# Spectral mixing plus gated linear unit on one core: the third and fourth sums of the transform blocks made by accumulating DMAs of GpSimd

## The chip, the cores and the metric

One core of a Trainium2 chip. Its engines run side by side and each works through its own instructions in order: TensorE (PE, matrix products into PSUM), VectorE (DVE, elementwise), ScalarE (ACT, here copies and the layer norm's roots), GpSimd (POOL, here almost only the issue of DMAs), SyncE (SP, issue of DMAs only). Sixteen DMA engines move the data; POOL's DMAs go through one queue (q0 of the profile), SP's through another (q1). The metric is the device time of one execution in microseconds.

## What is computed

```python
def _A_ref(x, dft_seq_re, dft_seq_im, dft_hid_re, dft_hid_im):
    a = jnp.einsum("bsd,ed->bse", x, dft_hid_re)
    b = jnp.einsum("bsd,ed->bse", x, dft_hid_im)
    y = jnp.einsum("ts,bse->bte", dft_seq_re, a) - jnp.einsum("ts,bse->bte", dft_seq_im, b)
    return y

def _B_ref(x, W_gate, W_up, W_down):
    gate = jnp.einsum("bsd,df->bsf", x, W_gate)
    up = jnp.einsum("bsd,df->bsf", x, W_up)
    gate = gate * (gate > 0)
    return jnp.einsum("bsf,fd->bsd", gate * up, W_down)

xn = _layernorm(x, axis=-1)
return x + _A_ref(xn, ...) + _B_ref(xn, ...)
```

Here x is 2048 tokens by 640, the sequence transforms are 2048 by 2048, and W_gate and W_up are 640 by 1728; everything is float32. The change lies in the product of the sequence transforms (`dft`) with the normalized tokens.

## The kernel before

**Precision.** Every float32 operand is split into a high part, a copy rounded to fp32r on ACT, and a low part, the difference, on DVE (`split`, L124 to L126). A product is three matmuls, L131 to L133. A matmul has a moving operand of 512 columns.

**Fewer products.** The product of the transforms with the tokens is a 2 by 2 block product, with the real and imaginary transform as one pair of blocks and the two halves of the tokens as the other. It is done with seven block products in place of eight (the scheme of Strassen and Winograd). For that, sums of transform blocks are needed, called T1 to T4, beside the plain blocks B11, B21 and B22. The sums of token blocks are made once, in `sums_124` and `sums_3`. The sums of results are made in `combine`.

**Chunks and units.** The 2048 output tokens are four chunks (c = 0 to 3) of 512. After the products of B11 and B21 for all chunks comes the stream of chunks 0 to 3. A chunk is twenty units: T1, T2, B22, T3 and T4, each for g = 0 to 3 (256 tokens of the half each). T31 is below the unit of T3 with g = 1. The units of a chunk run in the order T10 T11 T12 T13 T20 B220 T21 B221 T22 T23 B222 B223 T30 T31 T32 T33 T40 T41 T42 T43. A unit of T1 or B22 has 18 matmuls on PE, one of T2, T3 or T4 has 12.

A unit (`stream`) has a load, a preparation and its products. The load brings one or two transform blocks of 512 KB by SP (`get`, L690): for T1 the block (0, 0) into a `raw` tile and (1, 0) into a `tk` tile, `TK[g]`, for T2 the block (1, 1) into a `raw` tile, `ST[g]`; T3 loads (0, 0) a second time and T4 (0, 1), each into a `raw` tile of its own. The preparation subtracts on DVE (L686): T1 leaves its difference in `TK[g]`, T2 replaces it by `ST[g] - TK[g]`, T3 and T4 put the difference with `TK[g]` into their own `raw` tile, and B22 takes `ST[g]` as it is. Then the result is split into `cb`, of which there are three buffers. There are six `raw` and four `tk` buffers. So the next chunk's `tk` load (`tk<-in_dft`) waits for the last use of `TK[g]`, which is T4's subtraction.

**What sets the order.** `drive` goes through the list of units: the load of a unit runs some units ahead of its preparation, the preparation two units ahead of the products. `defer(n, f)` calls f n units later. A scheduler then lays out each engine's instructions by modelled times, so that steps can change places with those of neighbouring units; the order on an engine is fixed when the kernel is built.

**What else runs there.** For the second part of the kernel, token sets are made in the stream of chunks 0 to 2 (`token_sets`, six steps): POOL loads `rows` and `in_xt` into `st` tiles (L409, L410, L426, L427), DVE works on them (L432 to L439), and POOL stores them into `set1` (L416, L448), two stores of 512 KB for each of the last four steps. SP later loads sets back (`st<-set`, L762), and ACT and DVE split them into `r1` (`r<-st`). POOL also loads `sa` (L707) and stores the chunk's results (`pq`, L659). All DMAs of POOL stand in one order, and so do those of SP.

```python
                tc.keep_in_program_order(tt(part(ab, i), part(ab, i), part(mr, 0), op=OP.add))
...
            for i, st in ((B11, t["ab"]), (T1, t["mr"])):
                nc.gpsimd.dma_start(sets[q][i : i + 4, :, cs].rearrange("i p t -> p i t"),
                                  st.rearrange("p (i t) -> p i t", i=4))
```

Of the kernel before, what the change touches and what calls it, by code (L numbers as in the profile page):

```python
# [10 lines left out]
OP = mybir.AluOpType  # L11
# [10 lines left out]
NH = NG // 2  # L22
# [13 lines left out]
B11, B12, B21, B22, T1, T2, T3, T4, X4 = range(9)  # L36
# [23 lines left out]
def fnet_reglu_kernel(  # L60
# [15 lines left out]
    nc = tc.nc  # L76
# [41 lines left out]
    def stage():  # L118
        return stages[-1].tile([P, W2], F32, name="st")

    def copy(o, i):
        return nc.scalar.activation(o, i, AF.Copy)  # L122

    def split(hi, lo, src):  # L124
        nc.scalar.activation(hi, src, AF.Copy)  # L125
        return nc.vector.tensor_tensor(lo, src, hi.bitcast(F32), op=OP.subtract)  # L126
# [11 lines left out]
    @contextmanager  # L138
    def in_turn():

        with ExitStack() as order:
            if len(lows) > BACK:
                order.enter_context(tc.issue_after(lows[-BACK].ins))
            yield
# [5 lines left out]
    def defer(units, f):  # L150

        deferred.setdefault(now[0] + units, []).append(f)
# [300 lines left out]
    def raw():  # L453
        return raw_p.tile([P, W2], F32, name="raw")

    def parts():
        return ring.tile([P, 2, SG, CH], F32R, name="cb")

    def flat(t, v):
        return t[:, v].rearrange("p j t -> p (j t)")  # L460

    def s4_part(g):

        if "s4" not in late:
            late["s4"] = get_gw0().rearrange("p v z -> p (v z)")
        b = g * SG * 2 * HC
        return late["s4"][:, b : b + SG * 2 * HC].rearrange("p (j v d) -> p j v d", j=SG, v=2)

    def sums_124(g):


        def make():
            both = lambda g, cs: [xn_block(g, cs, v) for v in range(2)]
            a11, a21, a12, a22 = both(g, K1), both(g, K2), both(g + NH, K1), both(g + NH, K2)
            s1, s2 = (i.rearrange("p (j d) -> p j d", j=SG) for i in (lambda t: (t[:, :CH], t[:, CH:]))(stage()))
            w = s4_part(g)
            tt = nc.vector.tensor_tensor
            f = lambda i: i.bitcast(F32)
            tc.keep_in_program_order(tt(s1, f(a21[0]), f(a22[0]), op=OP.add))
            tt(s1, s1, f(a22[1]), op=OP.add)  # L480
            tt(s2, s1, f(a11[0]), op=OP.subtract)
            tt(s2, s2, f(a11[1]), op=OP.subtract)
            split(*a21, s1)

            tt(s1, f(a12[0]), s2, op=OP.subtract)
            tt(s1, s1, f(a12[1]), op=OP.add)
            split(*a11, s2)
            split(w[:, :, 0], w[:, :, 1], s1)

        todo.append((idle, make, idle, idle))  # L490
# [19 lines left out]
    E, F, TK, ST = {}, {}, {}, {}  # L510
# [40 lines left out]
    def resident(g, d):  # L551
        return lambda j, i: xn_part(g * SG + j, d + i)

    def fourth(g):
        return lambda j, i: tuple(s4_part(g)[:, j, v, i * P : (i + 1) * P] for v in range(2))

    def add(o, i0, i1):
        return nc.vector.tensor_tensor(o, i0, i1, op=OP.add)  # L558

    def minus(o, i0, i1):  # L560
        return nc.vector.scalar_tensor_tensor(o, i0, -1.0, i1, op0=OP.mult, op1=OP.subtract)  # L561

    def sums_a():
        return sums.tile([P, 3, CH], F32, name="sa")

    def sums_b():
        return sums.tile([P, 4, CH], F32, name="sb")
# [86 lines left out]
    def combine(c, name):  # L654

        a, b = F["a"], F.get("b")
        if name == "T1":
            F["b"] = b = sums_b()
        store = lambda m, at, t: defer(1, lambda: nc.gpsimd.dma_start(pqd[c][m][:, at : at + t.shape[1]], t))  # L659
        for i in range(2):  # L660
            p1, p5, u2 = a[:, i], b[:, i], b[:, 2 + i]
            e1, e2 = (E.get((k, i)) for k in ("e1", "e2"))
            if name == "T1":
                copy(p5, e2)
            if name == "T2":
                minus(u2, e1, p1)
            if name == "B22":
                nc.vector.tensor_tensor(u2, u2, e2, op=OP.subtract)
            if name == "T3":
                add(p1, e1, p1)  # L670
                minus(p5, p5, p1)
            if name == "T4":
                add(p1, e2, p1)
        if name == "B22":
            v = a[:, 2]
            minus(v, E["v2"], v)
            store(1, 0, b[:, 2:4])
            store(1, 2, a[:, 2:3])
        if name == "T3":
            store(1, 3, b[:, :2])  # L680
        if name == "T4":
            store(0, 3, a[:, :2])

    def stream(c, name, g):
        t = {}
        sub = lambda o, i0, i1: nc.vector.tensor_tensor(o, i0, i1, op=OP.subtract)  # L686

        def get(m, half, o=None):
            o = raw() if o is None else o
            late["dma"] = nc.sync.dma_start(o, dft[c, m, half * NH + g]).ins  # L690
            return o

        def load():
            if name == "T1":
                t["s"] = get(0, 0)
                TK[g] = get(1, 0, tk.tile([P, W2], F32, name="tk"))
            elif name == "T2":
                ST[g] = get(1, 1)
            elif name == "T3":
                t["s"] = get(0, 0)  # L700
            elif name == "T4":
                t["s"] = get(0, 1)

        def prepare():
            if name == "T2" and g == 0:
                F["a"] = sums_a()
                nc.gpsimd.dma_start(F["a"], firsts[c])  # L707
            src = t.get("s", TK[g])
            with in_turn():
                if name == "T1":  # L710
                    src = TK[g]
                    sub(src, src, t["s"])
                elif name == "T2":
                    sub(src, ST[g], src)
                elif name == "B22":
                    src = ST[g]
                elif name == "T3":
                    sub(src, TK[g], src)
                elif name == "T4":

                    sub(src, src, TK[g])
                t["b"] = b = parts()
                lows.append(split(flat(b, 0), flat(b, 1), src))

        def run():
            b = t["b"]
            es = lambda n: [(n, 0), (n, 1)]
            if name == "T1":
                product(g, b, resident(g, 2), es("e2"), True, False, ("v2", 0, True))
            elif name == "T2":  # L730
                product(g, b, resident(g, 0), es("e1"), True, False)
            elif name == "B22":
                product(g, b, fourth(g), es("e2"), False, True, ("v2", 1, False))
            elif name == "T3":
                product(g, b, resident(g + NH, 0), es("e1"), False, True)
            else:
                product(g, b, resident(g + NH, 2), es("e2"), True, False)

        todo.append((load, prepare, run, lambda: combine(c, name) if g == NH - 1 else None))

    def set_parts(q, i):
# [96 lines left out]
    tt = nc.vector.tensor_tensor  # L838
# [527 lines left out]
```

## Time and profile before

| | us |
|---|---|
| median of 3 runs (1026.6 to 1027.81) | 1027.18 |
| span of the profiled execution | 1025.6 |
| PE busy | 1019.3 (99%) |
| DVE busy | 805.5 (79%) |
| ACT busy | 448.2 (44%) |
| POOL busy | 96.9 (9%) |
| DMA queue of SP, share of the 16 engines | 47.9% |
| DMA queue of POOL, share of the 16 engines | 18.9% |

The span is what one profiled execution took from its first to its last instruction; the runs are timed from outside, and their median is 1.6 us above it. Times within the execution (as "314.15") count from the span's start. The streams of chunks 1, 2 and 3 lie at about 190 to 255, 255 to 320 and 320 to 385 us. In the rows of a timeline the brackets give the time for which the engine stood idle before the instruction and what ended it. Busy times don't say what waits for what; for that the chain of waits and the timelines are read.

### The profile page before, as it was taken

How to read it: one execution, taken by the hardware profiler on the slowest of the kernel's cores; microseconds unless marked ns; L12 is line 12 of the kernel's file. 1: busy time of each engine (PE TensorE's matmuls, PEld its weight loads, DVE VectorE, ACT ScalarE, POOL GpSimd, SP SyncE). 2: the span in 40 equal slices, each digit the busy share in tenths (PEclk: the TensorE clock that was granted, in tenths of full speed). 3: DMA queues.
4: the chain of work that ended last, by engine and by line, in shares of the span. 5: the costliest groups of instructions: out<-in, count | busy, mean ns of one | idle time of the engine just before them, and what ended most of it. 6: DMA issues, size and time to landing. Idle time of an engine off the chain costs nothing.

```text
span 1025.6 us, 12560 instructions
## 1 busy us (share of the span) xinstructions
PE 1019.3 (99%) x4525; PEld 843.1 (82%) x4525; DVE 805.5 (79%) x1113; ACT 448.2 (44%) x571; POOL 96.9 (9%) x161
## 2 busy tenths in 40 slices
PE   9999999999999999999999999999999999999998
PEld 7888888888888888888888888888888888888886
DVE  7967976969888797787887888876586779777776
ACT  6664453333334443433335544443454434553442
POOL 2000010121110001421110000000000001000000
PEclk9999999999999999999999999999999999999999
DMA  9884744976869665863474666664595747994655
GB/s 327 321 283 157 264 152 138 338 246 208 350 205 336 228 197 196 265 229 135 172 242 146 224 216 226 236 226 170 198 357 188 254 145 237 385 337 140 218 172 160
DMA packets 104542, 236.45 MB, mean 231 GB/s; under 512 B 11936, under 2 KB 55328, under 8 KB 102944
## 3 DMA queue, kind: packets, MB, share of 16 engines
q1 hardware_dynamic: 86896, 165.49, 47.9%
q0 software_dynamic: 17152, 69.74, 18.9%
q8 instruction: 35, 0.57, 0.2%
q10 hardware_dynamic: 432, 0.43, 0.1%
q14 instruction: 27, 0.22, 0.1%
HBM read 179.50 MB, written 55.07 MB: 229 GB/s over the span
## 4 chain that ended last, share of the span: by engine, by line
PE 97%; DVE 2%; DMA 0%; ACT 0%; issue 0%; SPq 0%; ACTq 0%
PE ps L132 31%; PE ps L131 31%; PE ps L133 31%; PE ps L519 3%; PE ps L548 1%; PE ps L1250 1%; DVE cb L126 1%; DMA raw<-in_dft 0%; DVE raw L686 0%; DVE r L126 0%; DVE sb L561 0%; DVE sa L558 0%; DVE tk L686 0%; ACT cb L125 0%; ACT cb L349 0%
## 5 line engine op out<-in xcount | busy, mean ns | idle before, releaser
L133 PE MATMUL ps<-cb,wt 128*128 128x512 f32 x412 | 160.0, 388 | 0.0
L132 PE MATMUL ps<-cb,wt 128*128 128x512 f32 x412 | 159.9, 388 | 0.0
L131 PE MATMUL ps<-cb,wt 128*128 128x512 f32 x412 | 159.8, 388 | 0.0
L125 ACT ACTIVATE cb<-rw 128x1024 fp32r<-128x1024 f32 x83 | 81.9, 987 | 121.7 <-PE ps L133 105.8
L126 DVE TENSOR_TENSOR cb<-rw,cb 128x1024 fp32r<-128x1024 f32 x83 | 94.0, 1132 | 50.9 <-ACT cb L125 50.5
L125 ACT ACTIVATE cb<-raw 128x1024 fp32r<-128x1024 f32 x64 | 67.8, 1060 | 103.7 <-PE ps L133 94.8
L126 DVE TENSOR_TENSOR cb<-raw,cb 128x1024 fp32r<-128x1024 f32 x64 | 78.2, 1221 | 31.9 <-ACT cb L125 31.6
L131 PE MATMUL ps<-xs_early,gw 128*128 128x512 f32 x260 | 101.1, 389 | 0.0
L132 PE MATMUL ps<-xs_early,gw 128*128 128x512 f32 x260 | 101.1, 389 | 0.0
L133 PE MATMUL ps<-xs_early,gw 128*128 128x512 f32 x260 | 101.1, 389 | 0.0
L133 PEld LDWEIGHTS ps<-cb,wt 128*128 128x128 f32 x412 | 77.3, 188 | 16.1 <-DVE wt L126 0.3
L131 PEld LDWEIGHTS ps<-cb,wt 128*128 128x128 f32 x412 | 77.3, 188 | 16.1
L132 PE MATMUL ps<-cb,xs_late 128*128 128x512 f32 x232 | 90.5, 390 | 0.1
L132 PEld LDWEIGHTS ps<-cb,wt 128*128 128x128 f32 x412 | 77.3, 188 | 15.9
L131 PE MATMUL ps<-cb,xs_late 128*128 128x512 f32 x232 | 90.3, 389 | 0.0
L133 PE MATMUL ps<-cb,xs_late 128*128 128x512 f32 x232 | 90.3, 389 | 0.0
L132 PE MATMUL ps<-cb,xs_early 128*128 128x512 f32 x226 | 87.9, 389 | 0.0
L131 PE MATMUL ps<-cb,xs_early 128*128 128x512 f32 x226 | 87.9, 389 | 0.0
L133 PE MATMUL ps<-cb,xs_early 128*128 128x512 f32 x226 | 87.9, 389 | 0.0
L122 ACT ACTIVATE gw<-z 128x1024 fp32r<-128x1024 f32 (+1 forms) x52 | 56.1, 1109 | 41.3 <-PE ps L133 29.4
L122 ACT ACTIVATE u<-ps 128x512 f32<-128x512 f32 x52 | 31.2, 599 | 89.6 <-PE ps L133 77.8
L867 DVE TENSOR_TENSOR gw<-z,gw 128x1024 fp32r<-128x1024 f32 (+1 forms) x52 | 64.8, 1284 | 2.9 <-ACT gw L122 2.8
(200 smaller groups left out, 1955.8 us busy)
## 6 DMA issues: line engine op xcount, KB each, us to landing
raw<-in_dft SPq DMA_DIRECT2D x94, 512.0 KB, 5.7
wt<-wparts SPq DMA_DIRECT2D x70, 256.0 KB, 3.2
z<-in_wgu SPq DMA_DIRECT2D x26, 640.0 KB, 4.6
hd<-ob POOLq DMA_DIRECT2D x26, 512.0 KB, 3.7
wparts<-pw POOLq DMA_DIRECT2D x12, 1024.0 KB, 4.1
rw<-hd SPq DMA_DIRECT2D x24, 512.0 KB, 5.9
tk<-in_dft SPq DMA_DIRECT2D x16, 512.0 KB, 8.1
rw<-pq SPq DMA_DIRECT2D x16, 512.0 KB, 6.3
```

The lines of the kernel that those rows point to most:

```text
L122: return nc.scalar.activation(o, i, AF.Copy)
L125: nc.scalar.activation(hi, src, AF.Copy)
L126: return nc.vector.tensor_tensor(lo, src, hi.bitcast(F32), op=OP.subtract)
L131: nc.tensor.matmul(ps, wh, mh, start=first, stop=False, skip_group_check=more)
L132: nc.tensor.matmul(ps, wh, ml, start=False, stop=False, skip_group_check=more)
L133: nc.tensor.matmul(ps, wl, mh, start=False, stop=last, skip_group_check=more)
L519: nc.tensor.matmul(E[0, key], xn_part(n * SG + j, d)[v == 1], b[:, int(v == 2), j], start=False, stop=n % NH == NH - 1 and (j, v) == (SG - ...
L548: nc.tensor.matmul(E[c, key], xn_part(j, d)[v == 1], b[c][0][:, int(v == 2), j], start=j == 0 and v == 0, stop=False)
L867: tt(self.w[:, 1, cs], self.z[:, cs], self.w[:, 0, cs].bitcast(F32), op=OP.subtract)
L1250: nc.tensor.matmul(B[out], w[:, v, oo : oo + P], b, start=False, stop=u == len(units) - 1 and v == 1, skip_group_check=more)
```

## The change

T3 and T4 no longer load blocks of their own by SP, and DVE no longer makes their differences. One unit after T2's split, POOL issues a DMA that adds the block (0, 1) from HBM onto `TK[g]`; T4 then uses `TK[g]`. One unit after B22's split, it adds the block (1, 0) onto `ST[g]`; T3 then uses that `raw` tile (`onto`, L694 of the changed kernel). That is 8 accumulating DMAs of 512 KB in a chunk, 32 in all, in place of 32 loads by SP and 32 operations of DVE. Since a DMA can only add here, signs are moved: T1 and T2 are sums in place of differences, the token sums of `sums_124` change their signs, and `combine` adds where it subtracted and the other way round, with a plain subtraction (`less`) in place of `minus`. Everything else is as before; in the changed kernel the lines behind these places have numbers lower by up to 5.

```diff
@@ sums_124
-            tc.keep_in_program_order(tt(s1, f(a21[0]), f(a22[0]), op=OP.add))
+            tc.keep_in_program_order(tt(s1, f(a22[0]), f(a21[0]), op=OP.subtract))
             tt(s1, s1, f(a22[1]), op=OP.add)
-            tt(s2, s1, f(a11[0]), op=OP.subtract)
-            tt(s2, s2, f(a11[1]), op=OP.subtract)
+            tt(s2, s1, f(a11[0]), op=OP.add)
+            tt(s2, s2, f(a11[1]), op=OP.add)
...
@@ combine
-    def minus(o, i0, i1):
-        return nc.vector.scalar_tensor_tensor(o, i0, -1.0, i1, op0=OP.mult, op1=OP.subtract)
+    def less(o, i0, i1):
+        return nc.vector.tensor_tensor(o, i0, i1, op=OP.subtract)
...
             if name == "T3":
-                add(p1, e1, p1)
-                minus(p5, p5, p1)
+                less(p1, p1, e1)
+                add(p5, p5, p1)
...
@@ stream
+        block = lambda m, half: dft[c, m, half * NH + g]
...
+        def onto(o, m, half):
+            nc.gpsimd.dma_start(o, block(m, half), accum_op=OP.add)
...
-            elif name == "T3":
-                t["s"] = get(0, 0)
-            elif name == "T4":
-                t["s"] = get(0, 1)
...
-            src = t.get("s", TK[g])
+            src = (ST if name in ("B22", "T3") else TK)[g]
             with in_turn():
                 if name == "T1":
-                    src = TK[g]
-                    sub(src, src, t["s"])
+                    add(src, src, t["s"])
                 elif name == "T2":
-                    sub(src, ST[g], src)
-                elif name == "B22":
-                    src = ST[g]
-                elif name == "T3":
-                    sub(src, TK[g], src)
-                elif name == "T4":
-                    sub(src, src, TK[g])
+                    add(src, ST[g], src)
                 t["b"] = b = parts()
                 lows.append(split(flat(b, 0), flat(b, 1), src))
+            if name == "T2":
+                defer(1, lambda: onto(src, 0, 1))
+            elif name == "B22":
+                defer(1, lambda: onto(src, 1, 0))
```

**POOL, chunk 2.** The DMAs of POOL from the last loads of token rows to the first store of chunk 2's results (`pq2`), before the change:

```order
L426 DMA st_2251<-rows_79 128x2x256
L427 DMA st_2252<-in_xt 128x2x256
L448 DMA set1_81<-st_2252 128x4x256
L448 DMA set1_81<-st_2251 128x4x256
L659 DMA pq2_88<-sb_2298 128x1024
```

and with it (L694 is the accumulation; `tk_2090` to `tk_2137` are `TK[0]` to `TK[3]`, `raw_2163` to `raw_2313` are `ST[0]` to `ST[3]`):

```order
L426 DMA st_2219<-rows_79 128x2x256
L427 DMA st_2220<-in_xt 128x2x256
L694 DMA tk_2090<-in_dft 128x1024
L694 DMA raw_2163<-in_dft 128x1024
L694 DMA tk_2109<-in_dft 128x1024
L694 DMA raw_2247<-in_dft 128x1024
L694 DMA tk_2129<-in_dft 128x1024
L694 DMA tk_2137<-in_dft 128x1024
L448 DMA set1_81<-st_2220 128x4x256
L448 DMA set1_81<-st_2219 128x4x256
L694 DMA raw_2289<-in_dft 128x1024
L694 DMA raw_2313<-in_dft 128x1024
```

Six accumulations now stand between the last load and the two set stores, two behind them, ahead of the store of results.

**ACT, chunk 2.** The high halves of the splits from T30 to T33, with those of the first two sets loaded back (`r1<-st`), before:

```order
L125 ACTIVATE cb_2427<-raw_2393 128x1024
L125 ACTIVATE cb_2453<-raw_2412 128x1024
L125 ACTIVATE r1_2674<-st_2675 128x1024
L125 ACTIVATE r1_2674<-st_2763 128x1024
L125 ACTIVATE cb_2477<-raw_2430 128x1024
L125 ACTIVATE cb_2500<-raw_2456 128x1024
```

and with the change:

```order
L125 ACTIVATE cb_2398<-raw_2163 128x1024
L125 ACTIVATE r1_2626<-st_2627 128x1024
L125 ACTIVATE cb_2421<-raw_2247 128x1024
L125 ACTIVATE r1_2626<-st_2717 128x1024
L125 ACTIVATE cb_2442<-raw_2289 128x1024
L125 ACTIVATE cb_2462<-raw_2313 128x1024
```

The first set's split has moved ahead of that of T31, the second's stays ahead of that of T32.

**DVE, chunk 2.** The same place on DVE, from T30's low half (`cb_2398`) to T32's (`cb_2442`), with the change:

```order
L126 TENSOR_TENSOR cb_2398<-raw_2163,cb_2398 128x1024
L126 TENSOR_TENSOR r1_2626<-st_2627,r1_2626 128x1024
L126 TENSOR_TENSOR cb_2421<-raw_2247,cb_2421 128x1024
L558 TENSOR_TENSOR sb_2268<-ps_2167,sb_2268 128x512
L558 TENSOR_TENSOR sb_2268<-ps_2168,sb_2268 128x512
L126 TENSOR_TENSOR r1_2626<-st_2717,r1_2626 128x1024
L561 TENSOR_TENSOR sa_2213<-sa_2213,ps_2181 128x512
L126 TENSOR_TENSOR cb_2442<-raw_2289,cb_2442 128x1024
```

The first set's low half, which before came behind T32's, now stands ahead of T31's (`cb_2421`), and the subtractions L686 between the splits are gone.

More of the change, by code (lines that the diff above doesn't have):

```diff
@@ L478, in make @@
             f = lambda i: i.bitcast(F32)
-            tc.keep_in_program_order(tt(s1, f(a21[0]), f(a22[0]), op=OP.add))
+            tc.keep_in_program_order(tt(s1, f(a22[0]), f(a21[0]), op=OP.subtract))
             tt(s1, s1, f(a22[1]), op=OP.add)
-            tt(s2, s1, f(a11[0]), op=OP.subtract)
-            tt(s2, s2, f(a11[1]), op=OP.subtract)
+            tt(s2, s1, f(a11[0]), op=OP.add)
+            tt(s2, s2, f(a11[1]), op=OP.add)
             split(*a21, s1)
-            tt(s1, f(a12[0]), s2, op=OP.subtract)
-            tt(s1, s1, f(a12[1]), op=OP.add)
+            tt(s1, s2, f(a12[0]), op=OP.subtract)
+            tt(s1, s1, f(a12[1]), op=OP.subtract)
             split(*a11, s2)
@@ L665, in combine @@
             if name == "T2":
-                minus(u2, e1, p1)
+                less(u2, p1, e1)
             if name == "B22":
-                nc.vector.tensor_tensor(u2, u2, e2, op=OP.subtract)
+                add(u2, e2, u2)
             if name == "T3":
-                add(p1, e1, p1)
-                minus(p5, p5, p1)
+                less(p1, p1, e1)
+                add(p5, p5, p1)
             if name == "T4":
@@ L675, in combine @@
             v = a[:, 2]
-            minus(v, E["v2"], v)
+            less(v, v, E["v2"])
             store(1, 0, b[:, 2:4])
@@ L685, in stream @@
         t = {}
-        sub = lambda o, i0, i1: nc.vector.tensor_tensor(o, i0, i1, op=OP.subtract)
+        block = lambda m, half: dft[c, m, half * NH + g]
         def get(m, half, o=None):
             o = raw() if o is None else o
-            late["dma"] = nc.sync.dma_start(o, dft[c, m, half * NH + g]).ins
+            late["dma"] = nc.sync.dma_start(o, block(m, half)).ins
             return o
+        def onto(o, m, half):
+            nc.gpsimd.dma_start(o, block(m, half), accum_op=OP.add)
         def load():
```

## The prediction

> **What bounds the kernel now.** I read the head of the page first, then the chain of waits (start, length, what), then the timelines of the engines around the loads that change.
>
> ```profile
> span 1025.6 us, 12560 instructions
> PE 1019.3 (99%) x4525; PEld 843.1 (82%) x4525; DVE 805.5 (79%) x1113; ACT 448.2 (44%) x571; POOL 96.9 (9%) x161
> PEclk9999999999999999999999999999999999999999
> PE 97%; DVE 2%; DMA 0%; ACT 0%; issue 0%; SPq 0%; ACTq 0%
> ...
> 6.19 8.49 PE ps L548 x36
> ...
> 31.31 4.08 PE ps L519 x18
> ```
>
> TensorE (PE) is busy 1019.3 of 1025.6 us, and the chain shows its work starting at 6.19 us. So 1025.6 - 1019.3 = 6.3 us of idle time is, but for 0.1 us, the start. Its clock is full in all forty slices. A matmul costs 4.08 / 18 = 0.227 us. The change keeps the number of matmuls, so only 0.1 us can be won: far less than the 0.2% (2.05 us) that a measurement of this kernel tells from no change. The question is what the change makes PE wait for. The 2% of DVE in the chain are one stretch:
>
> ```profile
> 314.15 0.24 PE ps L133
> 314.42 0.57 ACT cb L125
> 315.01 1.23 DVE cb L126
> 316.24 1.14 DVE raw L686
> 317.37 1.14 DVE r L126
> ...
> 325.32 0.60 DVE sa L558
> ...
> 329.99 1.15 DVE cb L126
> 331.18 0.50 PE ps L132
> ```
>
> From 315 to 331 us DVE works without a gap and PE only just keeps up. Here, at the end of chunk 2, a delay reaches the end at once. A delay elsewhere has about one unit to spare.
>
> **The change, part by part.**
>
> **Work removed from DVE.** The third and fourth sums are 32 operations:
>
> ```profile
> L686 DVE TENSOR_TENSOR raw<-raw,tk 128x1024 f32<-128x1024 f32 x16 | 19.5, 1218 | 0.0
> L686 DVE TENSOR_TENSOR raw<-tk,raw 128x1024 f32<-128x1024 f32 x16 | 19.2, 1217 | 0.0
> L561 DVE SCALAR_TENSOR_TENSOR sb<-sb,sa 128x512 f32<-128x512 f32 x8 | 5.4, 685 | 0.0
> L558 DVE TENSOR_TENSOR sa<-ps,sa 128x512 f32<-128x512 f32 x16 | 10.7, 685 | 3.5 <-PE ps L133 3.5
> ```
>
> That is 38.7 us of DVE. PE hides it everywhere but in the stretch above, and with 0.1 us of PE idle to win it is worth nothing. It does shorten DVE's catching up after a stall. The signs swap one operation for another of the same length (the last two rows: 685 ns both), so they count as nothing. So do the 32 loads that leave SP's queue: PE covers them, and without that cover they would be a gain.
>
> **Work added to POOL's queue: 32 accumulating DMAs of 512 KB.** No row shows one. A plain copy is bounded by the queues:
>
> ```profile
> q0 software_dynamic: 17152, 69.74, 18.9%
> set<-st POOLq DMA_DIRECT2D x8, 512.0 KB, 3.7
> raw<-in_dft SPq DMA_DIRECT2D x94, 512.0 KB, 5.7
> ```
>
> POOL's queue (q0) moved 69.74 MB in 18.9% of the time of all 16 DMA engines: 0.189 x 1025.6 / 69.74 x 0.524 = 1.46 us for 512 KB when all engines work on it. An accumulation reads the block from HBM and the tile from SBUF, and writes the tile. Bounds, by that row: 1.46 us, if the second read is free; 4.4 us, three times that, if each of the three streams takes as long as a copy. If they went one at a time it would be the 5.7 us of a block's landing. I take two copies, 2.9 us, since there are two reads for one write. Issue on POOL takes less (0.55 us for a copy of 512 KB, `pq<-sb` below) and is hidden by the transfers.
>
> ```profile
> 255.00:320.00 65.00, 65.00 (x288) 53.81 (x288) 54.40 (x63) 23.95 (x25) 9.24 (x14) 1.00 0.77 288
> ```
>
> This is chunk 2, with the DMA engines' share in the last column but one: 0.77 of 65 us, 50.1 us. Eight of SP's loads go (8 x 1.46 = 11.7) and eight accumulations come (8 x 2.9 = 23.2): 61.6 us, a share of 0.95. The engines still hold it, but loads will stand in line.
>
> [...]
>
> **Place A: the last set stores of chunk 2.** POOL's queue is in order. Now six accumulations stand between the last `in_xt` load and the last two set stores. Rows of POOL's timeline, then of SP's, the landing of the tile `set` from 295 to 320 us, and rows of ACT's timeline:
>
> ```profile
> 287.29 0.73 POOL L427 DMA_DIRECT2D st<-in_xt  x1 [2.10 <-issue]
> 297.83 0.77 POOL L448 DMA_DIRECT2D set<-st  x1 [9.81 <-DVE st L439]
> 301.33 0.77 POOL L448 DMA_DIRECT2D set<-st  x1 [2.73 <-DVE cb L126]
> 311.50 0.55 POOL L659 DMA_DIRECT2D pq<-sb  x1 [9.40 <-DVE sb L668]
> 306.22 0.80 SPq L762 DMA_DIRECT2D st<-set  x2
> DMA to landing us min/median/max: 3.2/5.2/6.3
> 303.59 1.06 ACT L125 ACTIVATE cb<-raw 128x1024 fp32r<-128x1024 f32 x1 [1.71 <-PE ps L133]
> 307.67 1.06 ACT L125 ACTIVATE cb<-raw 128x1024 fp32r<-128x1024 f32 x1 [3.02 <-PE ps L133]
> 311.48 1.06 ACT L125 ACTIVATE r<-st 128x1024 fp32r<-128x1024 f32 x1 [2.75 <-DMA st<-set]
> ```
>
> Before, the stores go at 297.83 and, once the first has landed (297.83 + 3.2 = 301.0), at 301.33. SP reads them back at 306.22, right behind the landing of the second. The load takes 5.2 us (311.48 - 306.22), and ACT, which waited 2.75 us for it, splits it at 311.48.
>
> Now the accumulations start when the `in_xt` loads have gone, about 288, and six of them take 6 x 2.9 = 17.5 us: 305.5. The first store's own data take 1.5: 307.0. The second goes 0.3 later and lands after a median 3.7: 311.0. SP's load, queued there, goes at 311.1 instead of 306.2, 4.9 late; all later loads of SP stand behind it. With the engines at 0.95 I give it the longest latency of that row, 6.3, not the median: landed at 317.4.
>
> Who waits: the scheduler has also moved the split of this set one unit forward, ahead of that of T31 on ACT and on DVE. After the landing come the copy of `r` (1.06), its low half and T31's low half on DVE (1.14 each): T31's operands are there at 317.4 + 1.06 + 2 x 1.14 = 320.7. T31 is due on PE two units after the ACT row of 307.67: one of 18 matmuls (4.08) and one of 12 (2.72), 314.5. That is 6.2 us of PE idle. Then T32's low half stands on DVE behind two operations on `sb`, the second low half of `r` and one on `sa` (0.60 each, as the `sa` of 325.32, and 1.14 for the low halves): 3 x 0.6 + 2 x 1.14 = 4.1 against the 2.7 us of T31 on PE, so 1.4 more. Removed subtractions let DVE catch up behind that. **Sum: 6.2 + 1.4 - 0.1 = 7.5 us.** Without the queue's delay the new order alone would cost at most that 1.4 and some tenths, since the old landing, 311.48, gives T31's operands at 314.8.
>
> [...]
>
> **Place B: reloads of TK at the chunk borders.** T4 now reads TK itself, so the tile comes free later.
>
> ```profile
> 247.75 0.33 SPq L690 DMA_DIRECT2D tk<-in_dft  x1
> 251.91 1.07 ACT L125 ACTIVATE cb<-raw 128x1024 fp32r<-128x1024 f32 x1 [1.66 <-PE ps L133]
> 253.00 1.22 DVE L126 TENSOR_TENSOR cb<-raw,cb 128x1024 fp32r<-128x1024 f32 x1
> tk<-in_dft SPq DMA_DIRECT2D x16, 512.0 KB, 8.1
> DMA to landing us min/median/max: 4.4/8.1/12.3
> ```
>
> Before, the load of TK0 goes at 247.75, behind T40's subtraction; now behind T40's low half, 253.00 + 1.22 = 254.2. The next chunk's T10 addition waits for it, and T43's low half stands behind this on DVE. T43 is due at 265.5 (251.91 plus three units of 2.72 for T43's ACT copy, plus two for the operands' lead). Less 2 x 1.14 us, the load may land as late as 263.2, a latency of 9.0. The rows of `tk` give 8.1 (median), in a queue that now has fewer loads: I take 0, with 12.3 - 9.0 = 3.3 us per border, 10 us for three, as the far end.
>
> **Place C: chunk 1.** There too the accumulations share POOL with set stores.
>
> ```profile
> 236.49 0.77 POOL L448 DMA_DIRECT2D set<-st  x1 [9.86 <-DVE st L439]
> 240.50 0.77 POOL L448 DMA_DIRECT2D set<-st  x1 [3.24 <-DVE sb L561]
> 249.19 1.06 ACT L125 ACTIVATE cb<-raw 128x1024 fp32r<-128x1024 f32 x1 [1.66 <-PE ps L133]
> ```
>
> From about 226, five accumulations, store, accumulation, store and the last accumulation (for T33) take 7 x 2.9 + 2 x 1.46 = 23.3 us: 249.3. T33's split ran at 249.19, and its operands are needed two units (5.4 us) later, less 2.3 for the split: 252.3. I take 0. At 4.4 us each it is 7 x 4.4 + 2.9 = 33.7, ready 259.7: 7.4 late.
>
> **Sum:** 1025.6 + 7.5 = 1033.1 for the profiled execution. The runs' median is 1027.18, 1.6 above its span, so **1034.7 us**.
>
> **Rivals.**
> - **Not slower: an accumulation costs little more than a copy.** At 1.46 us six end at 288 + 8.8 = 296.8, before the first store is ready at 297.83. The stores keep their times; left is the new order, at most 1.4 and some tenths: 1027.2 to 1029.2, within 0.2%. For it: the second read is from SBUF, not from HBM. Against it: a DMA engine still has to take both streams in. It decides up to about 1.4 copies, where six still end at 300.3.
> - **Much slower: three streams, 4.4 us each.** At Place A six end at 288 + 26.4 = 314.4, first store landed 315.9, second 319.9, the set's load 13.8 late instead of 4.9: 7.5 + 8.9 = 16.4. Place C adds 7.4, together 24: about 1051. By the share of chunk 2 it is 50.1 - 11.7 + 35.2 = 73.6 us of engine time in 65, the DMA engines themselves the bound by 8.6 us in this chunk alone. For it: POOL already waits 2.10 us at "issue" at 287.29, so its queue is short of room. [...]
> - **TK reloads stall at the borders** (Place B) by up to 3.3 us each, on top of Place A: about 1045. For it: 12.3 as the longest latency. Against it: the median is inside the 9.0.
> - **Faster: DVE's relief shows.** The chain from 315 to 331 loses its subtractions; the price is the 0.1 us of PE idle. Nothing more is there to win.
>
> **How the numbers follow.** Place A at about two copies: 0.50; as cheap as a copy: 0.19; three streams: 0.21; TK reloads: 0.07; faster for a reason I don't see: 0.03. Between the cases the price of an accumulation runs without a jump, from 1029 at 1.4 copies over 1034.7 at 2 to 1051 at 3; the likeliest case's own range is 1030 to 1040. The range of 8 in 10 goes from no change, 1026.4, to 1056, where 4.4 us and a late TK load at one or two borders come together (1051 + 3 to 7). Faster 0.03, same 0.19, slower 0.78.
>
> **What would show it.** Right: a PE idle of 4 to 8 us between 314 and 323 us and no other; ACT's copy `r<-st` waiting for the load of `set`, at about 317; the set stores of L448 at about 302 to 308, behind six accumulations that follow one another by 2.5 to 3 us; DVE's busy time about 39 us less. Wrong: accumulations that follow one another by 1.5 us with the stores at their old times, or PE idle at 252 to 256 us (Places B and C), which would mean a price of three streams or late TK loads.

## The result and the profile after

The changed kernel takes 1044.34 us (median of 4 runs, 1041.48 to 1045.85), the kernel before 1026.89 beside it: 17.45 us more, a ratio of 1.0164 with a 95% interval of 1.0147 to 1.018. The forecast was slower by 7.5 us, to 1034.7. The direction was right and the size less than half.

The head of the page of the changed kernel, its chain of waits by engine, and POOL's DMA queue:

```profile
span 1042.4 us, 12586 instructions
PE 1026.0 (98%) x4525; PEld 847.7 (81%) x4525; DVE 771.1 (74%) x1081; ACT 448.1 (43%) x571; POOL 125.3 (12%) x193
...
PEclk9999999999998999999999999999999999999999
...
q0 software_dynamic: 21760, 86.52, 27.8%
...
PE 90%; issue 4%; DMA 2%; DVE 2%; POOL 1%; ACT 0%; POOLq 0%; SPq 0%; DVEq 0%; ACTq 0%
```

DVE has 34.4 us less to do (forecast: about 39), and nothing came of it. PE now shares the chain with DMA and POOL, and with 4% of "issue". One slice of the clock's line is an 8. The queue gives the price of an accumulation: it took 0.278 x 1042.4 = 289.8 us of all engines, before 0.189 x 1025.6 = 193.8; put down to the 32 accumulations, the difference of 96.0 us is **3.0 us each**. The forecast had taken 2.9 against 1.46 for a copy.

The loss lies in two places. This is the view by windows (PE's busy time and matmuls come first; the last three columns are the granted clock, the DMA engines' share and GB/s):

```profile
251.00:264.00 13.00, 8.86 (x29) 6.11 (x28) 5.42 (x6) 4.02 (x5) 4.91 (x7) 0.87 0.78 203
264.00:320.00 56.00, 56.00 (x248) 46.36 (x247) 38.87 (x46) 17.11 (x17) 14.41 (x19) 1.00 0.81 238
320.00:336.00 16.00, 8.96 (x25) 6.46 (x24) 8.54 (x9) 6.01 (x6) 1.40 (x3) 0.68 0.95 292
```

At 0.227 us each, 29 matmuls are 6.6 us of 13.0, and 25 are 5.7 of 16.0. The start times of the matmuls locate it: PE loses 6.8 us from 251.3 to 263.1 and 10.6 from 320.7 to 335.1, 17.4 together. Between them it has no gap. Besides idling, PE was granted 0.87 and 0.68 of its clock in these two windows.

**First place, the end of chunk 1** (Place C of the prediction, which it took as 0). POOL's timeline:

```profile
235.31 0.88 POOL L694 DMA_DIRECT2D tk<-in_dft  x1 [1.57 <-DVE st L439]
240.33 0.80 POOL L448 DMA_DIRECT2D set<-st  x1 [4.14 <-issue]
242.83 0.85 POOL L694 DMA_DIRECT2D raw<-in_dft  x1 [1.71 <-issue]
247.37 0.81 POOL L448 DMA_DIRECT2D set<-st  x1 [3.69 <-DVE sa L561]
251.64 0.85 POOL L694 DMA_DIRECT2D raw<-in_dft  x1 [3.46 <-issue]
```

From 236 us POOL issues four DMAs in 16 us and stands ahead of them for 4.14, 1.71, 3.69 and 3.46 us. "issue" means that it waited for nothing that the profile shows (the 3.69 are put down to DVE, but the chain of waits has them as "issue" too). By the landings in the trace each of the four goes 0.3 to 0.4 us after an earlier DMA of POOL has landed: 239.98, 242.53, 247.03 and 251.38. So a set store waited while two accumulations were under way, and an accumulation while a set store and another accumulation were. The last accumulation, T33's, is issued at 251.64. ACT's timeline has the splits of T32 and T33, both behind their accumulations:

```profile
251.48 1.06 ACT L125 ACTIVATE cb<-raw 128x1024 fp32r<-128x1024 f32 x1 [8.21 <-DMA raw<-in_dft]
257.26 1.06 ACT L125 ACTIVATE cb<-raw 128x1024 fp32r<-128x1024 f32 x1 [4.72 <-DMA raw<-in_dft]
```

By the forecast's reckoning T33's split was needed by 252.3; it starts at 257.26, 5.0 us late. T32's is late too: PE waits 2.1 us for T32's operands and 3.3 for T33's, 5.4 in this place.

**Second place, the end of chunk 2** (Place A). POOL's timeline, the load of the sets on SP, and ACT:

```profile
294.73 0.93 POOL L694 DMA_DIRECT2D tk<-in_dft  x1 [1.75 <-DVE tk L558]
...
295.98 1.45 POOL L694 DMA_DIRECT2D tk<-in_dft  x1
300.49 0.83 POOL L694 DMA_DIRECT2D raw<-in_dft  x1 [3.06 <-DVE cb L126]
303.20 0.84 POOL L694 DMA_DIRECT2D tk<-in_dft  x1 [1.88 <-DVE st L432]
305.71 0.86 POOL L694 DMA_DIRECT2D tk<-in_dft  x1 [1.67 <-DVE st L439]
311.63 0.80 POOL L448 DMA_DIRECT2D set<-st  x1 [5.06 <-DVE sb L561]
315.99 0.79 POOL L448 DMA_DIRECT2D set<-st  x1 [3.56 <-issue]
```

```profile
319.44 0.86 SPq L757 DMA_DIRECT2D st<-set  x2
```

```profile
325.41 1.06 ACT L125 ACTIVATE r<-st 128x1024 fp32r<-128x1024 f32 x1 [14.11 <-DMA st<-set]
```

Everything stands 6.8 us later than before because of the first place. Taking that off, the stores go at 304.8 and 309.2 (forecast: 305.5 and 307.3; before: 297.8 and 301.3), and the set's split starts at 318.6 (forecast 317.4). ACT waited 14.11 us for it, with T31's split behind it in ACT's order. PE idles 8.1 us here. POOL waits for room here as well, whatever engine the brackets name: the fourth accumulation goes at 300.49, behind the first one's landing at 300.18, the next two at 303.20 and 305.71, behind landings at 302.94 and 305.41, and the first store at 311.63, behind one at 311.28.

**And then the clock.** The chain of waits behind that idle time (start, length, what):

```profile
328.92 0.80 PE ps L132
329.71 0.43 PE ps L133
...
334.40 0.39 PE ps L132
334.80 0.24 PE ps L133
```

Twelve matmuls follow each other by 0.43 us in place of 0.227 until 334.4: 2.4 us more, with all operands there. At the first place it is 6.8 - 5.4 = 1.4 us. By windows the granted clock was 0.52 from 259.60 to 263.10 us and 0.50 from 328.90 to 334.60. The prediction had no term for this; here both stalls cost more than their idle time.

### The profile page after: what moved, and what is told of

Same layout as the page of the kernel before. It is cut to its first block, busy times and chain, and to the rows that moved or that the text cites. A ratio compares the mean times of both kernels' runs of the same rounds, so it can differ in the third digit from the quotient of the medians.

```text
span 1042.4 us, 12586 instructions
## 1 busy us (share of the span) xinstructions
PE 1026.0 (98%) x4525; PEld 847.7 (81%) x4525; DVE 771.1 (74%) x1081; ACT 448.1 (43%) x571; POOL 125.3 (12%) x193
## 4 chain that ended last, share of the span: by engine, by line
PE 90%; issue 4%; DMA 2%; DVE 2%; POOL 1%; ACT 0%; POOLq 0%; SPq 0%; DVEq 0%; ACTq 0%
PE ps L132 29%; PE ps L133 29%; PE ps L131 28%; PE ps L519 3%; DVE cb L126 1%; PE ps L548 1%; DMA tk<-in_dft 1%; PE ps L1245 1%; DMA st<-set 1%; DMA raw<-in_dft 1%; PE ps L113 0%; DVE tk L558 0%; ACT cb L125 0%; POOL tk L694 0%; DMA set<-st 0%
## 5 line engine op out<-in xcount | busy, mean ns | idle before, releaser
L131 PE MATMUL ps<-cb,xs_late 128*128 128x512 f32 x232 | 92.4, 398 | 9.0 <-ACT cb L125 9.0
L126 DVE TENSOR_TENSOR cb<-raw,cb 128x1024 fp32r<-128x1024 f32 x48 | 58.5, 1223 | 53.8 <-ACT cb L125 53.7
L132 PE MATMUL ps<-cb,xs_late 128*128 128x512 f32 x232 | 92.6, 399 | 2.2 <-DVE cb L126 2.2
L133 PE MATMUL ps<-cb,xs_late 128*128 128x512 f32 x232 | 91.8, 396 | 0.0
L125 ACT ACTIVATE cb<-tk 128x1024 fp32r<-128x1024 f32 x48 | 50.8, 1060 | 84.4 <-PE ps L133 63.1
L125 ACT ACTIVATE cb<-raw 128x1024 fp32r<-128x1024 f32 x48 | 50.6, 1058 | 80.5 <-PE ps L133 62.6
L126 DVE TENSOR_TENSOR cb<-tk,cb 128x1024 fp32r<-128x1024 f32 x48 | 58.5, 1221 | 30.8 <-ACT cb L125 30.5
```

The costliest lines, as they stand in the source:

```text
L131: nc.tensor.matmul(ps, wh, mh, start=first, stop=False, skip_group_check=more)
L132: nc.tensor.matmul(ps, wh, ml, start=False, stop=False, skip_group_check=more)
L133: nc.tensor.matmul(ps, wl, mh, start=False, stop=last, skip_group_check=more)
```

## The experiments

Each run's median stands beside the median of the kernel before from the same chip; the ratio's 95% interval is in brackets. "Loss" of a place is worked out from the start times of its matmuls in the profiled execution, less 0.227 us for each.

**e1, the signs alone.** All moved signs stay; T3 and T4 load and add as before:

```diff
+            elif name == "T3" and True:
+                t["s"] = get(0, 0)
+            elif name == "T4" and True:
+                t["s"] = get(0, 1)
...
+                elif name == "T3" and True:
+                    less(src, TK[g], src)
+                elif name == "T4" and True:
+                    add(src, src, TK[g])
...
+            if True:
+                return
             if name == "T2":
                 defer(1, lambda: onto(src, 0, 1))
```

> The signs and token sums as in the change, but the accumulating DMAs left out: T3 and T4 load their block by SP and DVE makes the sum, as before. Theory (the accumulations in POOL's queue cost the 17 us): the time of before, 1026 to 1028.5 us, no PE idle at 250 to 330 us. Rival (the moved signs or the scheduler's new order of splits cost it): 1035 us or more.

1027.25 against 1027.21 us, ratio 0.9999 (0.9989 to 1.0008), no idle time of PE after the start. The signs and the new forms of the operations cost nothing; it is the accumulations. That a DMA can only add, for which the signs were moved, is a premise that no run tests.

**e2, copies in place of accumulations.**

```diff
-            nc.gpsimd.dma_start(o, block(m, half), accum_op=OP.add)
+            nc.gpsimd.dma_start(o, block(m, half))
```

> The changed kernel, each accumulating DMA made a plain copy of the same 512 KB at the same place of POOL's queue (the sums of T3 and T4 are left out by that). Theory (an accumulation takes the DMA engines 2.5 us and more, a copy about 1.5): copies follow one another by about 1.5 us, the set stores go near their old times, PE idles under 2 us in all; 1027 to 1030 us. Rival (it is the place in POOL's queue, with its waits for room, whatever the transfer costs): two thirds or more of the loss stay, 1038 us or more.

1028.98 against 1027.21 us, ratio 1.0017 (1.0008 to 1.0027). PE loses 1.7 us, from 314.6 to 319.7, and nothing in chunk 1. So the place in POOL's queue alone costs little: that is the forecast's "at most 1.4 and some tenths" for the new order of splits. The rest of the loss needs what an accumulation takes beyond a copy. That is time on the DMA engines: POOL's queue took 0.240 x 1027.0 = 246.5 us, so by the same reckoning these copies are 1.65 us each. And it is room: the fourth copy in chunk 2 goes at 290.36, before the first has landed (291.70), where the change's fourth accumulation waited for a landing. This run does not separate the two.

**e3 and e4, more room for POOL's queue.** The number by which the kernel sets the room of POOL's queue (`dynamic_dma_scratch_size`; the expectations call it the room for descriptors), four times as large, in the changed kernel and in the one before (part of one line):

```diff
-dynamic_dma_scratch_size=1024
+dynamic_dma_scratch_size=4096
```

> The changed kernel with four times the room for the descriptors of POOL's queue (dynamic_dma_scratch_size 4096 in place of 1024); same order on every engine. Theory (in chunk 1 the accumulations and set stores took turns in a queue with too little room: POOL's waits at 'issue' of 4.1, 1.7, 3.7 and 3.5 us from 236 to 252 us): these waits go, the addend of T33 lands at about 251 instead of 257, the PE idle near 250 to 263 us goes or falls below 2 us, that near 315 to 328 us shrinks only by what POOL gained there; 1033 to 1038 us. Rival (the DMA engines are full, room doesn't matter): 1042 to 1046 us as in the change.

> The kernel before with the larger room for descriptors alone, the control to the run before it. Both theories: no PE idle to win, 1026 to 1028 us; POOL's waits at 'issue' shorter. Anything faster than 1025 us would mean that the room bounded the kernel before as well.

The changed kernel 1039.71 us, ratio 1.0121 (1.0106 to 1.0136); the control 1035.07, ratio 1.0076 (1.0061 to 1.0091), both against 1027.21. The control missed both theories: it is 8 us slower. Its chain of waits has the reason, far from the change:

```profile
734.25 0.24 PE ps L133
734.50 0.33 SPq L1143
734.88 4.31 DMA wr<-in_hid
739.21 0.85 ACT wt L125
```

A load of the second part is issued only behind PE's last matmul there (734.25) and costs 8.2 us. e3 has the same idle time, so the two are to be compared with each other: 4.6 us apart, in place of 17. In chunk 1 of e3 PE has no gap; at the end of chunk 2 it loses 4.3 us. The waits for room make the whole of the first place and more than half of the second. That the larger room moves other tiles in memory, so that `wr` shares space with something PE still reads, fits the row but was not tried.

**e5 and e6, one chunk without accumulations**, by the edit of e1 with `c == 1` and with `c == 2` in place of `True`.

> The change in chunks 0, 2 and 3 only; in chunk 1 the sums of T3 and T4 are made by DVE from blocks that SP loads. Theory (two separate jams in POOL's queue: one in chunk 1, worth 6.9 us at 250 to 263 us, one at the end of chunk 2, worth 10.5): the first goes, the second stays as it is, 1036 to 1039 us. Rival (one jam that builds up from chunk 1 on and is only paid twice): the second shrinks as well, 1031 us or less.

> The change in chunks 0, 1 and 3 only; in chunk 2 the sums of T3 and T4 are made by DVE. Theory (two jams): the PE idle near 250 to 263 us as in the change, none near 315 to 328 us: 1033 to 1035.5 us. Rival (the jam moves on into chunk 2, since its token sets are late by then): 1037 us or more.

Without them in chunk 1: 1038.17 us against 1027.69, ratio 1.0106 (1.0091 to 1.0121). The first place is gone; the second stays, with stores at 307.98 and 311.87 and 13.3 us lost in the profiled execution. That execution was the slowest of four (1040.65; the others 1037.41 to 1038.67), so this place seems to vary by some 2 to 3 us. Without them in chunk 2: 1033.89 us, ratio 1.0055 (1.004 to 1.007), 6.5 us lost from 251.3 to 263.0 and about 1.2 in small gaps from 326 to 339. Two jams, each with its own time, as the theory had it; 10.5 and 6.2 add up to 16.7 of 17.45.

**e7, half of the accumulations.** T3's stay, T4 loads and adds as before:

```diff
+            elif name == "T4":
+                t["s"] = get(0, 1)
...
+                elif name == "T4":
+                    add(src, src, TK[g])
...
-            if name == "T2":
-                defer(1, lambda: onto(src, 0, 1))
-            elif name == "B22":
+            if name == "B22":
                 defer(1, lambda: onto(src, 1, 0))
```

> Half of the change: T3's sums by accumulating DMAs (four per chunk), T4's by DVE from blocks that SP loads. Theory (the loss comes from what stands ahead of the set stores and from the room of the queue, so it isn't proportional): two accumulations ahead of the last set stores in place of six, no idle in chunk 1; 1028 to 1032 us. Rival (each accumulation costs its share, 17 / 32 us): 16 of 32, 1035 to 1037 us.

1034.44 us, ratio 1.0062 (1.0045 to 1.0079): above what the theory gave, and near the rival's lower end. But the loss does not lie where a price per accumulation would put it: none in chunk 1, all 7.4 us at 314 to 325. POOL's timeline and ACT's there:

```profile
298.22 0.81 POOL L448 DMA_DIRECT2D set<-st  x1 [6.99 <-DVE st L439]
301.79 0.79 POOL L448 DMA_DIRECT2D set<-st  x1 [2.77 <-DVE cb L126]
302.57 0.97 POOL L694 DMA_DIRECT2D raw<-in_dft  x1
307.00 0.88 POOL L694 DMA_DIRECT2D raw<-in_dft  x1 [3.46 <-DVE cb L126]
```

```profile
312.32 1.06 ACT L125 ACTIVATE r<-st 128x1024 fp32r<-128x1024 f32 x1 [7.29 <-DMA st<-set]
315.91 1.06 ACT L125 ACTIVATE r<-st 128x1024 fp32r<-128x1024 f32 x1 [2.52 <-DMA st<-set]
316.87 2.93 ACT L125 ACTIVATE cb<-raw 128x1024 fp32r<-128x1024 f32 x3
```

The stores go at their old times. But in this kernel the scheduler puts the splits of both sets ahead of T31's, and the second set, loaded beside two accumulations, is there at 315.91 in place of 312.97. T31, due at 314.5, waits for both. So a late store is not even needed: the order of these splits makes PE depend on the sets' loads.

**e8, T4's accumulations behind the set stores.**

```diff
         def onto(o, m, half):
-            nc.gpsimd.dma_start(o, block(m, half), accum_op=OP.add)
+            with tc.issue_after(late["keep"]) if o is TK[g] and "keep" in late else ExitStack():
+                nc.gpsimd.dma_start(o, block(m, half), accum_op=OP.add)
...
-                defer(1, lambda: onto(src, 0, 1))
+                defer(9 + (g == 0), lambda: onto(src, 0, 1))
...
-                nc.gpsimd.dma_start(sets[q][i : i + 4, :, cs].rearrange("i p t -> p i t"),
-                                  st.rearrange("p (i t) -> p i t", i=4))
+                late["keep"] = nc.gpsimd.dma_start(sets[q][i : i + 4, :, cs].rearrange("i p t -> p i t"),
+                                                   st.rearrange("p (i t) -> p i t", i=4)).ins
```

> All 32 accumulations, but those onto TK are issued behind the set stores of their chunk on POOL (an order on that queue alone), since T4 needs them only then; two accumulations stay ahead of the last stores in place of six. Theory (the order in the queue): the last set stores go at about 298 and 302 us, the set is back at about 312, the idle near 315 to 328 us falls from 10.5 to at most 3 us; in chunk 1 T33 and T40 get their operands just in time; 1028 to 1033 us. Rival (the number of transfers counts, wherever they stand): 1040 us or more.

1052.16 us, ratio 1.0236 (1.0221 to 1.0251): far worse, against both. In chunk 2 the theory's part came true: taking off the 14.6 us lost by then, the stores go at 297.9 and 301.5, and the loss from 328.7 to 331.7 is 2.3 us. But in chunk 1 the accumulation onto `TK[3]` now stands behind four loads of token rows and two stores of results, most of them waiting at "issue":

```profile
257.38 0.55 POOL L659 DMA_DIRECT2D pq<-sa  x1 [2.62 <-issue]
261.59 0.72 POOL L427 DMA_DIRECT2D st<-in_xt  x1 [3.66 <-issue]
...
267.53 0.92 POOL L695 DMA_DIRECT2D tk<-in_dft  x1 [1.20 <-issue]
```

T43 waits for it, 14.6 us lost from 262.6 to 282.9. Another 7.7 are lost at 348 to 358, behind a load of `tk` that goes at 338.37 and takes 13.36 us to land; this second stall is Place B's, with later accumulations onto `TK`.

**e9, the sets' loads later.** The first two loads of sets keep behind the transform loads that precede them in the program:

```diff
-                with ExitStack() if get else tc.issue_after(late["dma"]):
+                with tc.issue_after(late["dma"]):
                     nc.sync.dma_start(t[i], sets[q][i])
```

> The change with one more order on SP's queue: the first two loads of sets (st<-set) stand behind the transform loads that come before them in the program, so that the scheduler puts the splits of these sets behind T40's and T41's, not ahead of T31's and T32's; POOL's queue as in the change, six accumulations ahead of the set stores. Theory (at the end of chunk 2 it is the split of the late set, standing ahead of T31's, that stops PE): the idle near 315 to 328 us goes though the stores are as late as before; left is chunk 1's, 6 to 7 us: 1032.5 to 1035.5 us. Rival (the accumulated tiles themselves are late there): 1040 us or more.

1040.16 us against 1027.27, ratio 1.0129 (1.0112 to 1.0146); the profiled execution was the fastest of four, 1037.28. In it the second place falls from 10.6 to 2.9 us, while the stores are as late as in the change, 310.56 and 315.41; the first place stays at 6.7. So most of that loss needs the set's split ahead of T31's. Of the 2.9 us left, 2.2 are the rival's part: T32's accumulation, behind the late stores, makes ACT wait 8.15 us at 324.02. The other three executions took 2.7 to 4.3 us more, and no trace shows where; by the medians this kernel loses 12.9 us, the change 17.45.

**e10, the same with twice the room** (2048).

> The same with twice the room for POOL's descriptors (2048). Theory (chunk 1's idle comes from the waits for room): that idle goes as well or falls below 2 us; 1026.5 to 1029 us if the larger room leaves the rest of the program alone, and up to 8 us more if the load wr<-in_hid near 734 us is late again, as with 4096. Rival (twice the room is not enough, or the engines are full): 1032 us or more with the idle at 250 to 263 us still there.

1027.02 against 1027.27 us, ratio 0.9999 (0.999 to 1.0008). All 32 accumulations are there, and PE has no gap above 0.11 us. POOL's timeline in chunk 2:

```profile
297.47 0.86 POOL L694 DMA_DIRECT2D tk<-in_dft  x1 [2.31 <-DVE cb L126]
298.10 1.02 POOL L448 DMA_DIRECT2D set<-st  x1
299.54 0.80 POOL L448 DMA_DIRECT2D set<-st  x1 [0.41 <-DVE st L439]
```

Same order on the queue, six accumulations ahead, and the stores go at 298.10 and 299.54. Here POOL waits for its operands and not for room. It does not beat the kernel before, as PE had nothing to win.

**e11 and e12, a stall of DVE's making in the kernel before**, to measure the clock by itself. The low half of one split (T12, chunk 1) is written four or eight times more:

```diff
+                for _ in range(4 if (c, name, g) == (1, "T1", 2) else 0):
+                    lows[-1] = sub(flat(b, 1), src, flat(b, 0).bitcast(F32))
```

> The kernel before, with the low half of one unit's split (T12 of chunk 1) written four times more by DVE, 4 x 1.14 us, so that PE has to wait there. For the clock: theory (PE runs at half rate for some us after a long idle time, and only then): an idle time of 1 to 2 us near 205 us, and matmuls 0.227 us apart again right behind it. Rival (the half rate in the change comes from the accumulating DMAs, not from idling): the same here, since nothing accumulates.

> The same, written eight times more, 8 x 1.14 us: an idle time of 4 to 7 us near 205 us. Theory (half rate after a long idle time): some 8 to 15 matmuls 0.427 us apart behind it, 1.5 to 3 us more than the idle time. Rival (half rate comes from the accumulating DMAs): matmuls 0.227 us apart at once.

One run each, 1030.84 and 1032.57 us. The chain of e11 behind two idle times of 0.68 and 1.35 us:

```profile
215.16 0.23 PE ps L131
215.39 0.41 PE ps L132
...
218.36 0.43 PE ps L133
218.79 0.24 PE ps L132
```

There is no accumulating DMA in this kernel, and PE runs at half rate for 3.4 us (215.39 to 218.79): 1.6 us lost beside 2.0 of idle. In e12 it is 1.4 us beside 4.8. So the half rate does not need accumulating DMAs; in all these traces it stands behind idle time. The length that the theory gave for it was wrong: 2.0 us in two pieces were enough, and the longer stall did not cost more. In e12 the half rate stands behind the first two pieces (0.68 and 1.41 us); behind the last and longest, 2.74 us, PE starts at full rate at 220.09.

**e13 and e14, twice the room alone**, in the changed kernel and in the one before.

> The changed kernel with twice the room for POOL's descriptors (2048) and nothing else. Theory (two causes that add: the room stops PE in chunk 1, the split of the late set ahead of T31's at the end of chunk 2): the idle near 250 to 263 us goes, 2 to 5 us are left near 314 to 322 us, as with four times the room: 1029.5 to 1032.5 us. Rival (the room alone): 1026.5 to 1028.5 us, no idle left.

> The control: the kernel before with twice the room. Both theories: 1026 to 1028.5 us, without the idle near 734 us that four times the room gave (it was in the layout of memory). If that idle is here, it has to be taken off the runs with twice the room as well.

1031.18 us, ratio 1.0034 (1.0021 to 1.0047), and 1026.62 us, ratio 0.9993 (0.9984 to 1.0003), both against 1027.55. The room alone takes 13.8 of the 17.45 us away; 3.6 are left, all from 313.9 to 320.9, where the two sets' splits stand. The issue of T33's accumulation in chunk 1, of the first accumulation and the last two set stores in chunk 2, and SP's load of the sets:

```profile
238.38 0.85 POOL L694 DMA_DIRECT2D raw<-in_dft  x1 [0.35 <-DVE sb L561]
...
283.54 0.97 POOL L694 DMA_DIRECT2D tk<-in_dft  x1
...
297.69 1.02 POOL L448 DMA_DIRECT2D set<-st  x1
299.12 0.80 POOL L448 DMA_DIRECT2D set<-st  x1 [0.41 <-DVE st L439]
```

```profile
306.69 0.86 SPq L757 DMA_DIRECT2D st<-set  x2
```

T33's accumulation lands at 248.74. The stores go at their old times, behind six accumulations that land 2.5 us apart (291.34 to 303.83), and the sets' load goes 0.5 us later than before (306.22). At the second place each remedy alone, the order (e9) or the room, takes about two thirds of the loss or more (10.6 falls to 2.9 and to 3.7 us), so there the two causes work together and do not simply add; both at once leave nothing (e10). The late `wr` load of e4 is not in e14.

## Why the prediction was right or wrong

**What bounds the kernel, and that nothing could be won: right.** e1, e10 and e14 show that neither DVE's nor POOL's relief brings a measurable gain.

**Removed work and signs at nothing: right** (e1).

**The price of an accumulation: right.** Two copies, 2.9 us, were taken; the queue shows 3.0, and in e13 the accumulations land 2.5 us apart. The reason given, two reads for one write, is not shown: no trace has the reads and the write of a transfer apart. The engines' share, forecast as 0.95 over the 65 us of chunk 2, was 0.92 in e10, where PE never stops (255 to 320 us); the 0.95 of the last window above is no sign of it, as the kernel before has 0.97 from 320 to 340 us. "Issue on POOL takes less and is hidden" holds, with 0.86 us as the median and not 0.55.

**Place A: right in kind; that the size agrees is in part luck.** Six accumulations ahead of two stores, a set that comes back late, its split ahead of T31's: 7.5 us forecast, 8.1 us idle in the profiled execution. But the forecast put the stores' delay down to the time of the transfers, six times 2.9 us from 288 on. In e13 the same DMAs stand in the same order with more room, the sets' load is 0.5 us late and not 4.9, and 3.7 us are lost in place of 10.6. So most of the delay was waiting for room here too; the sum had such a wait only between the two stores. The parts don't agree one by one either: T31 waited 8.1 us where 6.2 were forecast, and T32's 1.4 us don't show, as T31's matmuls at half rate covered them (in e13, at full rate, T32 waits 1.19 us). By itself (e5) the place is larger in its profiled execution, 11.1 us idle; there POOL's waits for room, 4.23 and 3.09 us ahead of the stores, put them at 307.98 and 311.87. e9 shows that the loss needs the split's place, e7 that the split can stop PE even with punctual stores.

**Place C, "I take 0": the step that failed.** It added up seven accumulations and two stores by their time on the DMA engines, 23.3 us, as if POOL could put them all in the queue and the engines work them off. POOL could not: with two accumulations under way there was no room for a set store, with a set store and an accumulation none for the next accumulation, and each was issued only when an earlier one had landed. So the latencies stood in a row, 5.5 to 9.0 us for each accumulation in this place, and T33's landed at 257.16 in place of 249.3. The trace of before had the sign, POOL's waits at "issue" of 2.10 us at 287.29 and others, and the prediction named it, but as an argument for the rival "three streams" and not as a price of its own. e3 and e13 settle it: with more room and nothing else changed, this place costs nothing, and in e13 T33's accumulation lands at 248.74, near the sum's 249.3. It is 6.8 of the 17.4 us. PE idle at 252 to 256 us stood in the prediction as a sign of three streams or of late TK loads; the idle came, and was neither.

**The clock: a term that was missing.** 3.8 of the 17.4 us are matmuls at half rate behind the two stalls. The prediction counted a stall by its length. At Place A not all of the 2.4 us are extra: T32's low half starts on DVE only at 332.25 and takes 1.14 us, and at full rate T31 would have been through at 331.4, so by an estimate from these rows PE would have waited some 1.7 us for T32 anyway. The prediction's statement that the clock is full in all slices was true of before and said nothing of a kernel that stalls.

So of 17.4 us: 8.1 at Place A where 7.5 were forecast, 5.4 at Place C where 0 was, and 3.8 of clock where no term stood.

**Place B: right for this kernel.** The loads of `tk` did not stop PE. e8 shows that the stall exists once an accumulation onto `TK` comes late.

**The rivals.** "TK reloads" has the nearest time, about 1045 against 1044, by chance: its cause did not occur. "Three streams", about 1051, was the one that had chunk 1 stop PE, but by the price of an accumulation, and it was the room. "As cheap as a copy" is what e2 shows, 1028.98 us, inside the 1027.2 to 1029.2 given for it.

**Not settled:** why executions of the changed kernel differ by 4 us (1041.48 to 1045.85) where those of before differ by 1.3; where the other three runs of e9 lost their 2.7 to 4.3 us; and when idle time of PE is followed by half rate and when not (e11 to e13).

## What to carry to other kernels

POOL's queue had two limits here, the time of its transfers and the room for those under way. Its waits at "issue", and others that end 0.3 us behind a landing whatever engine the profile names, were the second, and there latencies added (5.5 to 9.0 us for each accumulation at the end of chunk 1), not transfer times (3.0). Before work is moved to such a queue, look for these waits; here twice the room made the same 32 accumulations free once the order was mended. And where TensorE never idles, a forecast of a stall should ask for two terms, its length and the matmuls at half rate that may follow (here 5.4 and 1.4 us, 8.1 and 2.4).

## What was not expected of the hardware

- By the share of POOL's queue an accumulating DMA of 512 KB took 3.0 us of all 16 DMA engines, a copy 1.46 (1.65 for the copies of e2); its issue on POOL took 0.84 to 1.45 us (median 0.86), a copy's 0.55 (`pq<-sb`) or 0.77 (`set<-st`). With three accumulations under way the fourth was issued only behind a landing (300.49 behind 300.18); a fourth copy went with three under way (e2, 290.36).
- TensorE ran at 0.43 us per matmul behind idle times of 2.0 us in two pieces (e11, seven matmuls) and of 8.1 us (twelve), but at full rate behind 0.97, 1.22 and 1.19 us close together (e13) and behind 2.74 us (e12). The runs show no sharp bound.
- Four times the room for POOL's queue made the kernel before 8 us slower (1035.07 against 1027.21) by a late load at 734 us; twice the room changed nothing there (1026.62 against 1027.55).
